# Seven half products for eight in the second net's first multiplication, with all lead times planned anew

## The chip, the cores and the metric

The kernel runs on one core of a Trainium2 chip. The metric is the device time of one execution, in microseconds (us). Three runs of the kernel before gave 726.67, 730.49 and 735.12 us, a median of 730.49.

## The reference, cut to what matters

Attention, then two feed-forward nets, on 4 x 576 = 2304 tokens of width 512:

```
out_d     = attention on means of 4 tokens, repeated 4 times
out_local = attention within |i - j| < 4
x = (out_up + out_local), heads side by side          # 2304 x 512

h = x @ w_in                                          # first net, 512 -> 2048
x = (h * tanh(softplus(h))) @ w_out                   # 2048 -> 512

h  = x @ w_in2                                        # second net, 512 -> 1024
e  = exp(h - max(h)); sm = e / (sum(e) + 1e-9)
s  = h * sm
ln = (s - mean(s)) / sqrt(var(s) + 1e-6) * g_ln
out = ln @ w_out2                                     # 1024 -> 512
```

The weights come as 64-bit floats, everything else as 32-bit.

## The kernel before, in words

**Numbers in two parts.** Every large multiplication splits both operands into a high part that the fast multiplication format holds exactly and the rest (ScalarE copies the high part, VectorE subtracts it from the whole), and adds three of the four partial products (`PASS`). So one 128 x 128 x 512 block costs three matmuls.

**First net.** Tokens go in five blocks of 3 or 4 units of 128 (`BLOCKS`). For each block 16 chunks of 128 hidden features run, one per slot: `chunk_in` (12 matmuls, then a chain of ScalarE and VectorE operations, L659 to L676) and `chunk_out` (12 matmuls into `y`, L687). The attention of later blocks runs beside the chunks of earlier ones (`coarse` for the means of 4, `local` for the band; `NEXT` gives their lead). A block's result goes to DRAM (`block_end`, `yscr`). There are 80 slots.

**Second net's weights.** `second_decode` (16 parts of 128 x 512: the first eight are w_in2, the others w_out2 with `g_ln` multiplied in) unpacks the 64-bit words, and writes a part to DRAM (`wscr`). `second_split` loads two parts and splits them into a buffer with the tag `wi`; the eight buffers of that tag come free as the first net's weights are used for the last time, in the last block.

**Second net.** It runs over 18 tiles of 128 tokens. `tile_in` loads a tile's input from `yscr` (512 features over 128 partitions in 4 parts), splits it, and does 24 matmuls (4 parts x 2 halves of 512 outputs x 3 passes, L728) into one buffer of two PSUM banks (`y`). Then: maximum (L752), exponential with its sum (L754), product with h and its sum (L757, two halves), sum of squares (L765), a few values per token (L768 to L780), scaling (L793 on VectorE, L795 on ScalarE), a turn of the 128 x 1024 result by way of DRAM (`zscr`, one write and four reads) and VectorE's transposition of 32 x 32 blocks (L821), split (L824, L825). `tile_out` does 24 matmuls (8 parts x 3 passes, L837), copies the result out (L842) and stores it. A tile takes two buffers of the tag `wo`, of which there are eight: `ez` from the exponential to the split, `ln` from the split to the end of `tile_out`. Tiles 0 and 1 do their first multiplication beside the last block's chunks. The last tile is turned by TensorE (L804) in place of DRAM.

**The order.** `Plan` collects every operation with its engine, an estimated duration, a due time in slots (`want`), and what it reads and writes. `Plan.run` then plays the queues through with these estimates: whenever an engine is free, the operation with the lowest due time whose inputs and buffers are there is taken. A due time is thus a rank and holds nothing back. The order found is written into the program; each engine works it off in sequence, waiting where an input is not there. The numbers at the top of the file (`LEAD`, `EARLY`, `WANT`, `NEXT`, ...) set the due times. SP's queue carries most transfers, GpSimd's (POOL) the averaging loads of `coarse` and the adding writes of `block_end`.

```
dma(want + 0.2, lambda: wscr[i], x, r=[x], w=[wparts[i // 2]], nbytes=262144)
...
pe(24 * 0.216, s + (8 if t < 2 else G2LAG), g2, [ln] + [w4t[k][0] for k in range(8)], [o])
```

Of the kernel before, what the change touches and what calls it, by code (L numbers as in the profile page):

```python
# [47 lines left out]
LAG = 0.15  # L48
AHEAD = 2
# [40 lines left out]
class Plan:  # L90
# [30 lines left out]
    def run(self):  # L121
# [18 lines left out]
        while len(order) < len(ops):  # L140
            for eng, queue in ready.items():
                while at[eng] <= now:
# [22 lines left out]
                    if eng in ("sp", "pool"):  # L165
                        at[eng] = now + (0.45 if eng == "sp" else 1.1)
# [4 lines left out]
                        end = dma + ((1.3 if now < 150 else 4.0) if lag is None else lag)  # L171
# [37 lines left out]
def kernel(  # L209
# [47 lines left out]
    wscr = dr.tile([16, 128, 512], F32, name="wscr")  # L257
    zscr = dr.tile([NTI, 128, 1024], F32, name="zscr")
    yparts = [[Buf(None, None, None, 0) for _ in range(2)] for _ in range(NB)]
    wparts = [Buf(None, None, None, 0) for _ in range(8)]  # L260
# [15 lines left out]
    def pe(cost, want, fn, r, w, after=()):  # L276
        return op("pe", cost, want, fn, r, w, after=after)
# [337 lines left out]
    w3t = {}  # L615
    w4t = {}
# [18 lines left out]

    def second_split(j, want):
        w = S([128, 2, 2, 512], "wi", 8, F32R)
# [72 lines left out]
    def tile_in(t, s):  # L710
# [7 lines left out]
        dma(s - 2, xf, lambda: yscr[:, :, 128 * t:128 * t + 128], r=yparts[i] + ([] if first else yparts[NB - 2]) + wparts, w=[xf, x], nbytes=262144)  # L718
# [3 lines left out]
        for m in range(2):  # L722
# [8 lines left out]
            pe(12 * 0.216, s, g1, [x] + [w3t[c, m][0] for c in range(4)], [hs[m if first else 0]])  # L731
# [3 lines left out]
        zv = View(ez, lambda b: b[:, 0].rearrange("p (a f) -> p a f", a=4))  # L735
        zs = Buf(None, None, None, 0)
        e = lambda: ez()[:, 0].rearrange("t (m f) -> t m f", m=2)
        mv = S([128, 4], "mv", 2)
        r = S([128, 4], "r2", 2)
# [16 lines left out]
        for m in range(2):  # L756
# [31 lines left out]
        def turned(m):  # L788
# [4 lines left out]
        dve(dve_us(512), s + 0.4, lambda: nc.vector.tensor_scalar(  # L793
            turned(0), flat(0), mv()[:, 2:3], y(), op0=ALU.add, op1=ALU.mult), [mv, r], [ez])
        act(act_us(512), s + 0.4, lambda: nc.scalar.activation(  # L795
            turned(1), flat(1), AF.Identity, bias=c(), scale=y()), [r], [ez])
# [16 lines left out]
        dma(s + 0.5, lambda: zscr[t], lambda: ez()[:, 1], r=[ez], w=[zs], nbytes=524288, lag=0.3)  # L813
        for g in range(4):
            dma(s + 0.6, lambda g=g: zv()[32 * g:32 * g + 32],
                lambda g=g: zscr[t].rearrange("(a t) (g f) -> g t a f", a=4, g=4)[g],
                r=[zs, ez], w=[zv], nbytes=131072, join=True, lag=1.0)
# [11 lines left out]
    def tile_out(t, s, ln):  # L829
# [23 lines left out]
    dve(0.1, -99, lambda: nc.vector.memset(ones()[:, 1:2], 0.5), [], [ones])  # L853
    for t in sms:
# [55 lines left out]
    for k in range(8):  # L910
        second_split(k, 16 * NB - 16 + 2 * k + 2)
    for t in range(NTI):
        s = 16 * NB + (INTO[t] if t < 2 else 3 * (t - 2))
        tile_out(t, s, tile_in(t, s))
# [70 lines left out]
```

## Time and profile before

| | |
|---|---|
| median of 3 runs | 730.49 us (726.67 to 735.12) |
| profiled execution | 731.2 us, span 729.4 us |
| mean granted TensorE clock | 0.979 |
| TensorE matmul busy | 692.7 us (95%), 5584 instructions |
| VectorE busy | 458.0 us (63%) |
| ScalarE busy | 489.9 us (67%) |
| GpSimd busy | 71.3 us (10%) |
| mean transfer rate | 135 GB/s |

The span is the time from the first to the last instruction of one execution. Busy times of engines overlap. The first net with its attention fills the span to about 538 us; the second net's tiles the rest.

### The profile page before, as it was taken

Reading aid. Unit: us, or ns where it says so; the run is one execution under the profiler, and the core shown is the slowest. Engines: PE = TensorE matmul, PEld = TensorE weight load, DVE = VectorE, ACT = ScalarE, POOL = GpSimd, SP = SyncE. Lnnn points to the kernel's source line nnn. Section 1 sums busy time; section 2 is a strip of 40 time slices with the busy share of each in tenths; the row PEclk is TensorE's granted clock in tenths of the full one; section 3 lists DMA queues with packets and bytes.
Section 4 is the critical chain, followed back from the end, with each engine's and each line's share of the span. In section 5 each row is a group of like instructions: output and inputs, shape, how many; then the busy total and the mean of one; then the engine's idle time right before and its main releaser. Section 6 shows DMA issues by size and latency. Waiting matters only on the chain.

```text
span 729.4 us, 14381 instructions
## 1 busy us (share of the span) xinstructions
PE 692.7 (95%) x5584; PEld 583.3 (80%) x5584; DVE 458.0 (63%) x1008; ACT 489.9 (67%) x1159; POOL 71.3 (10%) x86
## 2 busy tenths in 40 slices
PE   3748999999999998999999999999999999999997
PEld 2546778999987787999778888888888788888886
DVE  6597987787655454655665647445556667667662
ACT  3877987887878675666776757677655555555552
POOL 2042351122311121000000000000000000000000
PEclk9959999999999998999999999999999999999999
DMA  8897875847445355242343323312234544444331
GB/s 250 250 235 201 233 183 114 269 107 170 90 106 139 76 123 135 86 153 75 108 134 96 105 73 113 119 44 85 75 111 120 173 162 142 143 161 136 129 126 44
DMA packets 75564, 98.35 MB, mean 135 GB/s; under 512 B 6568, under 2 KB 58152, under 8 KB 75496
## 3 DMA queue, kind: packets, MB, share of 16 engines
q1 hardware_dynamic: 63464, 83.61, 36.3%
q0 software_dynamic: 9440, 9.10, 8.9%
q10 hardware_dynamic: 2592, 4.72, 1.7%
q8 instruction: 44, 0.72, 0.4%
q14 instruction: 24, 0.20, 0.1%
HBM read 73.81 MB, written 23.59 MB: 134 GB/s over the span
## 4 chain that ended last, share of the span: by engine, by line
PE 84%; DMA 6%; DVE 3%; SPq 2%; ACT 2%; issue 1%; POOL 0%; POOLq 0%; ACTq 0%
PE y L687 26%; PE h L659 25%; PE at L837 13%; PE y L728 12%; DMA qkd<-in_qkc_dram 3%; SPq L268 2%; PE at L420 2%; PE at L728 1%; DMA qu<-in_qu_dram 1%; PE at L490 1%; PE at L358 1%; DMA vd<-in_vc_dram 1%; PE at L397 1%; PE at L539 1%; PE at L526 1%
## 5 line engine op out<-in xcount | busy, mean ns | idle before, releaser
L687 PE MATMUL y<-g,wo 128*128 128x512 f32 (+1 forms) x960 | 219.1, 376 | 0.0
L659 PE MATMUL h<-x,wi 128*128 128x512 f32 (+1 forms) x960 | 213.4, 373 | 2.1 <-DVE e L673 2.1
L659 PEld LDWEIGHTS h<-x,wi 128*128 128x128 f32 x960 | 174.2, 189 | 26.8 <-DVE e L673 3.3
L687 PEld LDWEIGHTS y<-g,wo 128*128 128x128 f32 x960 | 173.9, 190 | 24.4 <-issue 2.0
L837 PE MATMUL at<-wi,wo 128*128 128x512 f32 x432 | 100.6, 389 | 0.0
L837 PEld LDWEIGHTS at<-wi,wo 128*128 128x128 f32 x432 | 81.0, 188 | 16.8
L728 PE MATMUL y<-wi,raw 128*128 128x512 f32 x384 | 89.9, 390 | 1.1 <-DVE raw L720 1.1
L728 PEld LDWEIGHTS y<-wi,raw 128*128 128x128 f32 x384 | 71.9, 188 | 16.6 <-DVE raw L720 1.5
L667 ACT ACTIVATE e<-h 128x512 f32<-128x512 f32 (+1 forms) x80 | 44.2, 552 | 59.5 <-PE h L659 59.0
L673 DVE SCALAR_TENSOR_TENSOR e<-e,h 128x512 f32<-128x512 f32 (+1 forms) x80 | 50.3, 629 | 34.4 <-ACT e L672 33.9
L669 ACT ACTIVATE e<-e,ones 128x512 f32<-128x512 f32 (+1 forms) x80 | 54.5, 681 | 19.5 <-DVE e L668 18.9
L668 DVE TENSOR_SCALAR e<-e 128x512 f32<-128x512 f32 (+1 forms) x80 | 31.9, 399 | 51.7 <-ACT e L667 51.5
L676 DVE TENSOR_TENSOR g<-e,g 128x512 fp32r<-128x512 f32 (+1 forms) x80 | 50.7, 634 | 19.9 <-ACT g L675 19.1
L675 ACT CAST g<-e 128x512 fp32r<-128x512 f32 (+1 forms) x80 | 46.0, 574 | 24.3 <-DVE e L673 23.9
L671 ACT ACTIVATE e<-e,ones 128x512 f32<-128x512 f32 (+1 forms) x80 | 54.4, 680 | 1.7
L266 POOL DMA_DIRECT2D qkd<-in_qkc_dram x36 | 35.4, 1017 | 147.1 <-DMA qkd<-in_qkc_dram 77.7
L672 ACT ACTIVATE e<-e 128x512 f32<-128x512 f32 (+1 forms) x80 | 46.8, 585 | 1.1
L266 POOL DMA_DIRECT2D vd<-in_vc_dram x36 | 35.4, 1030 | 50.7 <-DMA vd<-in_vc_dram 45.9
L842 ACT COPY ys<-at 128x512 f32<-128x512 f32 x18 | 10.6, 589 | 38.5 <-PE at L837 38.5
L379 ACT ACTIVATE sm<-sm,nm 128x40 f32<-128x40 f32 x112 | 35.1, 316 | 0.7 <-DVE nm L373 0.6
L754 ACT ACTIVATE wo<-y,nm 128x1024 f32<-128x1024 f32 x16 | 17.9, 1118 | 22.3 <-DVE nm L752 22.3
L554 DVE TENSOR_SCALAR ys<-ys 128x512 int32<-128x512 int32 (+1 forms) x38 | 18.8, 495 | 19.7 <-ACT ys L553 19.3
(166 smaller groups left out, 803.0 us busy)
## 6 DMA issues: line engine op xcount, KB each, us to landing
raw<-in_w_dram SPq DMA_DIRECT2D x24, 512.0 KB
zscr<-wo SPq DMA_DIRECT2D x17, 512.0 KB
wo<-zscr SPq DMA_DIRECT2D x68, 128.0 KB
qkd<-in_qkc_dram POOLq DMA_DIRECT2D x36, 144.0 KB, 4.4
wi<-in_w_dram SPq DMA_DIRECT2D x5, 1024.0 KB
wo<-in_w_dram SPq DMA_DIRECT2D x5, 1024.0 KB
ku<-in_ku_dram SPq DMA_DIRECT2D x15, 320.0 KB
vu<-in_vu_dram SPq DMA_DIRECT2D x60, 80.0 KB
```

The source lines that it names most:

```text
L266: return op("pool", nbytes / DMA_RATE, want, lambda: nc.gpsimd.dma_start(out_(), in_(), accum_op=ALU.add), r, w, after=after)
L659: mm(h()[:, :N], w()[:, f % 2, a, 128 * c:128 * c + 128], x()[:, b, c, :N], start=(n == 0), stop=(n == 11))
L667: act(act_us(N), s + 0.1, lambda: nc.scalar.activation(e(), h()[:, :N], AF.Exp), [h], [eb])
L669: act(act_us(N, 0.09), s + 0.1, lambda: nc.scalar.activation(e(), e(), AF.Square, bias=ones()[:, 0:1]), [ones], [eb])
L671: lambda: nc.scalar.activation(e(), e(), AF.Ln, scale=0.5, bias=ones()[:, 1:2]), [ones], [eb])
L672: act(act_us(N), s + 0.1, lambda: nc.scalar.activation(e(), e(), AF.Exp, scale=-1.0), [], [eb])
L673: dve(dve_us(N), s + 0.2, lambda: nc.vector.scalar_tensor_tensor(e(), e(), 1.0, h()[:, :N], op0=ALU.subtract, op1=ALU.mult), [h], [eb])
L675: act(act_us(N), s + 0.2, lambda: nc.scalar.copy(g()[:, 0, :N], e()), [eb], [g])
L676: dve(dve_us(N), s + 0.2, lambda: nc.vector.tensor_tensor(g()[:, 1, :N], e(), g()[:, 0, :N].bitcast(F32), op=ALU.subtract), [eb], [g])
L687: mm(y[d2]()[:, d, :N], w()[:, f % 2, a, c:c + 128], g()[:, b, :N], start=(f == fs[0] and n == 0), stop=(f == fs[-1] and n == 2))
L728: mm(part(m), x()[:, a, c, :], w()[:, i, b, :], start=(n == 0), stop=(n == 11))
L837: mm(o(), ln()[:, a, k, :], w()[:, i, b, :], start=(n == 0), stop=(n == 23))
```

## The change

Tiles 2 to 15 are taken in pairs (`PAIRED`). Tile t is `xa`, tile t + 1 `xb`, the input features are cut into two halves and the outputs into two halves, so that a pair's first multiplication is a 2 x 2 by 2 x 2 product of blocks: eight half products, each 128 tokens x 256 features x 512 outputs, 6 matmuls. `pair_in` does it with seven (Strassen's scheme in Winograd's form): four sums of the inputs, four of the weights, seven products in four banks (both banks of a `y` buffer and both `h` banks), and sums of the products. Two of the products are added onto banks that hold an earlier product, after that one has been read.

- `weight_sums` makes the four sums of w_in2's blocks, in two halves, and writes them to `wscr` as eight more parts. `second_split` then runs for 12 pairs of parts; `HOMES` puts eight into `wi`, two into `wo` (of eight buffers) and two into the buffer `x0` of the first net's input, `SPLITS` gives order and due times.
- `pair_in` splits seven operands of 256 features (four blocks of input, of which two as one copy and one alone, and four sums). For every second pair, the first among them, they lie in `x1`, the input buffer of the last block; for the others in `raw`, `e` and `vu`. The results of the products are added into `c2` in SBUF, two by plain additions, four by an addition that also keeps the maximum. Exponential and product then read SBUF and not PSUM, 1024 wide; the second tile of a pair has later due times (`PSTEP`).
- `normal` is the rest of `tile_in`, now shared. The square of the scaled sum goes from VectorE (two operations) to ScalarE (one). In pairs both scalings are ScalarE's.
- `tile_out` takes its output buffer from `qu` and `ku`, and a lag of its own for the tiles of a pair (`PLAG`).
- The planner's estimates: TensorE 0.2267 us for a matmul of the second net in place of 0.216, 0.05 us more for any group on TensorE, 0.47 us more for a GpSimd transfer, other lags for the turn through DRAM. All numbers that set due times are new.

```
-LEAD = 2.2
-EARLY = -95.5
-CLOAD0 = -108.6
-VLOAD = [-115.1, -87.3]
-LOAD0 = -77.4
-FIRST = {'wi': (-67.7, -66.3), 'wo': (-64.9, -40.0)}
...
-NEXT = {0: (0.6, 7.5, -8.4, 0.2), 26: (-4.7, 4.4, -13.4, 0.2), 32: (-3.9, 7.5, -5.0, 1.7), 48: (1.4, 10.4, 2.8, 3.4)}
-WANT = [6.9, 4.6, 4.5, 5.8, -4.5, 13.8, 34.8, 28.7]
-G2LAG = 10
-INTO = (-7, -0.9)
+LEAD = 2.22
+EARLY = -97.3
+CLOAD0 = -101.34
+VLOAD = [-107.17, -83.16]
+LOAD0 = -80.26
+FIRST = {'wi': (-68.45, -50.57), 'wo': (-67.01, -47.07)}
...
+NEXT = {0: (0.03, 8.7, -23.77, 0.71), 26: (-3.98, 6.49, -13.57, 0.59), 32: (-3.63, 9.6, -1.34, 1.76), 48: (2.15, 11.88, 21.41, 28.49)}
+WANT = [11.64, 4.76, 5.17, 6.13, -17.51, 32.44, 46.22, 39.82]
+G2LAG = 35.66
+SUMS = (-4.62, 4.1)
+HOMES = ["wi"] * 6 + ["wo"] * 2 + ["x0"] * 2 + ["wi"] * 2
+SPLITS = ((8, -20.07), (9, -11.82), (0, -10.66), (1, -12.07), (2, -24.69), (3, 0.53), (10, 20.13), (11, 5.71), (6, 2.55), (7, 32.54), (4, -88.28), (5, 21.64))
+PAIRED = range(2, 16, 2)
+PLAG = (16.26, 16.41)
+XLOAD = -17.27
+XPREP = -37.01
+PSTEP = 45.84
+TERMS = [(0, 0, "11", False), (1, 5, "T2", False), (2, 3, "T3", False), (3, 4, "T1", False),
+         (0, 1, "21", False), (3, 6, "22", True), (2, 2, "T4", True)]
+INTO = (-26.71, -0.78)
+POOL_LAG = 0.47
...
-        return op("pe", cost, want, fn, r, w, after=after)
+        return op("pe", cost + 0.05, want, fn, r, w, after=after)
...
+    def weight_sums(c, want):
+        xs = [S([128, 2, 512], tag, 1) for tag in ("vu", "atT")]
+        for h in range(2):
+            dma(want - 2, xs[h], lambda h=h: wscr[2 * c + 4 * h:2 * c + 4 * h + 2].rearrange("i k n -> k i n"),
+                r=[wparts[c], wparts[c + 2]], w=xs, nbytes=524288, join=h > 0)
...
+        for out_, i0, i1 in (...):
+            dve(dve_us(512), want, lambda ...: nc.vector.tensor_tensor(
+                out_(), i0(), i1(), op=ALU.subtract), [], [a, b])
+        for h in range(2):
+            j = 8 + 2 * c + h
+            dma(want + 0.2, lambda j=j: wscr[2 * j:2 * j + 2].rearrange("i k n -> k i n"), xs[h], r=[xs[h]], w=[wparts[j]], nbytes=524288)
...
+    def pair_in(t, s, loads):
+        xp = S([128, 2, 4, 128], "ys", 2)
+        sums = S([128, 4, 2, 128], "atT", 1)
+        if t % 4 == 2:
+            x = S([128, 7, 2, 2, 128], "x1", 1, F32R)
+            cuts = [(0, 2), (2, 3), (3, 7)]
...
+        else:
+            cuts = [(0, 2), (2, 3), (3, 5), (5, 7)]
...
+        for o, i0, i1, f in (...):
+            dve(dve_us(256), s - XPREP, lambda ...: nc.vector.tensor_tensor(
+                sums()[:, o], i0(), i1(), op=f), xs, [sums])
+        for (a, b), home in zip(cuts, homes):
...
+            act(act_us(256 * (b - a)), s - XPREP, lambda src=src, home=home: nc.scalar.copy(home()[:, :, 0], src()), [buf], [home])
+            dve(dve_us(256 * (b - a)), s - XPREP, lambda src=src, home=home: nc.vector.tensor_tensor(
+                home()[:, :, 1], src(), home()[:, :, 0].bitcast(F32), op=ALU.subtract), [buf], [home])
...
+        yt = P("y")
+        banks = [View(yt, lambda b, m=m: b[:, m]) for m in range(2)] + [P("h"), P("h")]
+        def product(n, k, name, more):
...
+                for c in range(2):
+                    for a, b in PASS:
+                        w, m = ws[c]
+                        mm(banks[n](), home()[:, o, a, c, :], w()[:, m, b, :], start=(i == 0 and not more), stop=(i == 5), skip_group_check=more)
+                        i += 1
+            pe(6 * 0.2267, s, g1, [home] + [w for w, _ in ws], [banks[n]])
+        c2 = [S([128, 2, 512], "g", 3) for _ in range(2)]
...
+        def plus(out_, a, n, r=None, m=0, first=True):
+            if r is None:
+                dve(dve_us(512) + 0.1, s + 0.1, lambda: nc.vector.tensor_tensor(out_(), a(), banks[n](), op=ALU.add), [a, banks[n]], [out_])
+            else:
+                dve(dve_us(512) + 0.1, s + 0.1, lambda: nc.vector.tensor_tensor_reduce(
+                    out_(), a(), banks[n](), 1.0, LOWEST if first else r()[:, 1:2], ALU.add, ALU.max,
+                    r()[:, 1:2] if first else r()[:, 2:3]), [a, banks[n]], [out_, r])
...
+        go()
+        act(act_us(512), s + 0.1, lambda: nc.scalar.copy(ct[0](), banks[0]()), [banks[0]], [ct[0]])
+        go()
+        plus(u, ct[0], 1)
+        go()
+        plus(cu[1], u, 2)
+        go()
+        plus(cu[1], cu[1], 3, nms[1])
+        go()
+        plus(ct[0], ct[0], 0, nms[0])
+        go()
+        plus(ct[1], u, 3, nms[0], first=False)
+        go()
+        plus(cu[0], u, 2, nms[1], first=False)
+        for n in range(2):
+            nm, h, hs = nms[n], c2[n], (ct, cu)[n]
+            d = PSTEP * n
...
+            act(act_us(1024, 0.2), s + 0.2 + d, lambda ...: nc.scalar.activation(
+                ez()[:, 0], hv(), AF.Exp, bias=nm()[:, 0:1], accum_out=su()[:, 0:1]), hs + [nm], [ez, su])
+            dve(dve_us(1024) + 0.1, s + 0.3 + d, lambda ...: nc.vector.tensor_tensor_reduce(
+                ez()[:, 0], ez()[:, 0], hv(), 1.0, 0.0, ALU.mult, ALU.add, mv()[:, 0:1]), hs, [ez, mv])
...
+            lns.append(normal(t + n, s + d, ez, su, mv))
+        return lns
...
-            pe(12 * 0.216, s, g1, [x] + [w3t[c, m][0] for c in range(4)], [hs[m if first else 0]])
+            pe(12 * 0.2267, s, g1, [x] + [w3t[c, m][0] for c in range(4)], [hs[m if first else 0]])
...
-    def tile_out(t, s, ln):
+    def tile_out(t, s, ln, lag=None):
...
-        pe(24 * 0.216, s + (8 if t < 2 else G2LAG), g2, [ln] + [w4t[k][0] for k in range(8)], [o])
-        os_ = S([128, 512], "ys", 2)
+        pe(24 * 0.2267, s + (lag or (8 if t < 2 else G2LAG)), g2, [ln] + [w4t[k][0] for k in range(8)], [o])
+        os_ = S([128, 512], ("qu", "ku")[t % 2], 1)
...
-    for k in range(8):
-        second_split(k, 16 * NB - 16 + 2 * k + 2)
+    for c in range(2):
+        weight_sums(c, 16 * NB - 16 + SUMS[c])
+    for j, want in SPLITS:
+        second_split(j, 16 * NB - 16 + want)
```

## Rows read from the trace of the kernel before

**Rows 1.** Busy time by stretch: start:end, length, busy (instructions) by engine, clock, transfers.

```profile
0.00:125.00 125.00, 95.51 (x1288) 74.54 (x1289) 97.05 (x194) 92.82 (x280) 37.28 (x48) 0.90 0.80 214
...
520.00:729.40 209.40, 204.57 (x905) 168.66 (x903) 129.02 (x333) 107.69 (x202) 0.00 (x0) 1.00 0.39 128
```

**Rows 2.** The chain of waits in order of time: start, length, what.

```profile
588.75 5.44 PE y L728 x24
594.19 5.44 PE at L837 x24
...
714.75 10.93 PE at L837 x48
```

**Rows 3.** Busy time by stretch, two tiles of the steady part.

```profile
621.39:643.15 21.76, 21.76 (x97) 18.02 (x97) 14.49 (x38) 11.60 (x22) 0.00 (x0) 1.00 0.44 146
```

**Rows 4.** Groups by line and shape, 520 us on: busy, mean ns, idle before.

```profile
L757 DVE SCALAR_TENSOR_TENSOR wo<-wo,y 128x512 f32<-128x512 f32 x32 | 21.8, 681 | 4.4 <-ACT wo L754 3.8
...
L752 DVE TENSOR_REDUCE nm<-y 128x1 f32<-128x1024 f32 x16 | 19.6, 1222 | 10.8 <-PE y L728 10.7
...
L795 ACT ACTIVATE wo<-wo,r 128x512 f32<-128x512 f32 x17 | 13.9, 816 | 15.2 <-DVE r L780 15.0
...
L793 DVE TENSOR_SCALAR wo<-wo,mv,r 128x512 f32<-128x512 f32 x17 | 9.2, 539 | 0.0
...
L720 DVE TENSOR_TENSOR raw<-ku,raw 128x512 fp32r<-128x512 f32 x8 | 5.5, 690 | 1.7 <-ACT raw L719 1.7
L719 ACT CAST raw<-ku 128x512 fp32r<-128x512 f32 x8 | 4.9, 607 | 0.0
...
L772 ACT ACTIVATE r<-r 128x1 f32<-128x1 f32 x17 | 3.4, 201 | 0.9 <-DVE r L768 0.9
...
L757 DVE DVE_READ_ACCUMULATOR wo<-wo,y 128x1 f32 x32 | 2.6, 83 | 0.0
...
L762 DVE TENSOR_SCALAR su<-su 128x1 f32<-128x1 f32 x17 | 2.5, 149 | 0.0
L563 DVE TENSOR_TENSOR wi<-ys,wi 128x1024 fp32r<-128x1024 f32 x2 | 2.4, 1222 | 0.3 <-ACT wi L562 0.3
L562 ACT CAST wi<-ys 128x1024 fp32r<-128x1024 f32 x2 | 2.1, 1044 | 0.0
```

**Rows 5.** Groups of VectorE by line and shape, whole run.

```profile
L430 DVE TENSOR_TENSOR ys<-at,up 128x256 f32<-128x256 f32 x20 | 8.1, 420 | 9.5 <-PE at L420 9.2
...
L558 DVE SCALAR_TENSOR_TENSOR ys<-wi,ys 128x1024 int32<-128x1024 int32 x5 | 6.1, 1229 | 0.0
```

**Rows 6.** Instructions in order of time, one tile: start, length, what.

```profile
628.13 1.12 ACT L754 ACTIVATE wo<-y,nm 128x1024 f32<-128x1024 f32 x1 [1.25 <-DVE nm L752]
...
648.02 0.62 ACT L824 CAST wo<-wo 128x512 fp32r<-128x512 f32 x1 [0.26 <-DVE wo L821]
...
651.80 0.68 DVE L825 TENSOR_TENSOR wo<-wo 128x512 fp32r<-128x512 f32 x1
...
659.31 5.60 PE L837 MATMUL at<-wi,wo 128*128 128x512 f32 x24
```

**Rows 7.** Busy time by stretch, the last block of the first net.

```profile
420.00:540.00 120.00, 119.97 (x529) 98.81 (x528) 65.02 (x120) 81.76 (x134) 0.00 (x0) 1.00 0.25 80
```

**Rows 8.** Instructions of TensorE in order of time, where the nets meet.

```profile
527.25 5.60 PE L728 MATMUL at<-wi,raw 128*128 128x512 f32 x24
...
538.13 5.72 PE L728 MATMUL y<-wi,raw 128*128 128x512 f32 x24
```

**Rows 9.** One instruction of TensorE and its wait; busy time of the stretch.

```profile
278.68 1.22 PE L490 MATMUL at<-qkd 64*64 64x144 f32 x12 [2.19 <-DMA qkd<-in_qkc_dram]
...
276.00:292.00 16.00, 13.80 (x133) 12.34 (x132) 7.05 (x18) 8.79 (x31) 2.50 (x3) 0.79 0.49 124
```

**Rows 10.** Instructions of TensorE in order of time: the first large matmuls.

```profile
54.38 7.12 PE L659 MATMUL h<-x,wi 128*128 128x512 f32 x24
```

**Rows 11.** Waits from 520 us on: engine, line, for whom, total, times, longest.

```profile
DVE r L768 <- ACT wo L765: 31.7, 16, 2.5
```

More of the change, by code (lines that the diff above doesn't have):

```diff
@@ L170, in run @@
                         dma = max(dma, at[eng] + 1.2) + cost
-                        end = dma + ((1.3 if now < 150 else 4.0) if lag is None else lag)
+                        end = dma + (((1.3 if now < 150 else 4.0) + (POOL_LAG if eng == "pool" else 0.0)) if lag is None else lag)
                     else:
@@ L256 @@
     yscr = dr.tile([128, 4, NT], F32, name="yscr")
-    wscr = dr.tile([16, 128, 512], F32, name="wscr")
+    wscr = dr.tile([24, 128, 512], F32, name="wscr")
     zscr = dr.tile([NTI, 128, 1024], F32, name="zscr")
     yparts = [[Buf(None, None, None, 0) for _ in range(2)] for _ in range(NB)]
-    wparts = [Buf(None, None, None, 0) for _ in range(8)]
+    wparts = [Buf(None, None, None, 0) for _ in range(12)]
     def dma(want, out_, in_, r=(), w=(), nbytes=0, accum=False, after=(), pool=False, join=False, lag=None):
@@ L615 @@
     w3t = {}
+    wsum = {}
+    xsum = S([128, 2, 2, 2, 512], "x0", 1, F32R)
     w4t = {}
@@ L711, in tile_in @@
+    def tile_in(t, s, loads):
         i = max(n for n in range(NB) if starts[n] <= 128 * t)
@@ L717, in tile_in @@
         part = (lambda m: hs[m]()) if first else (lambda m: hs[0]()[:, m, :])
-        dma(s - 2, xf, lambda: yscr[:, :, 128 * t:128 * t + 128], r=yparts[i] + ([] if first else yparts[NB - 2]) + wparts, w=[xf, x], nbytes=262144)
+        dma(s - 2, xf, lambda: yscr[:, :, 128 * t:128 * t + 128], r=yparts[i] + ([] if first else yparts[NB - 2]) + wparts, w=[xf, x], nbytes=262144, after=loads[-1:])
         act(act_us(512), s - 1, lambda: nc.scalar.copy(x()[:, 0], xf()), [xf], [x])
@@ L791, in turned @@
             return ez()[:, 1].rearrange("t (g k f) -> t g k f", g=4, k=8)[:, :, 4 * m:4 * m + 4]
[L793 to L796, printed above, removed]
+        paired = t in PAIRED or t - 1 in PAIRED
+        if not paired:
+            dve(dve_us(512), s + 0.4, lambda: nc.vector.tensor_scalar(
+                turned(0), flat(0), mv()[:, 2:3], y(), op0=ALU.add, op1=ALU.mult), [mv, r], [ez])
+        for m in range(0 if paired else 1, 2):
+            act(0.82, s + 0.4, lambda m=m: nc.scalar.activation(
+                turned(m), flat(m), AF.Identity, bias=c(), scale=y()), [r], [ez])
         if last:
@@ L909 @@
         second_decode(k, s, [g1_op[s]])
-    for k in range(8):
-        second_split(k, 16 * NB - 16 + 2 * k + 2)
+    for c in range(2):
+        weight_sums(c, 16 * NB - 16 + SUMS[c])
+    for j, want in SPLITS:
+        second_split(j, 16 * NB - 16 + want)
+    for n in ("11", "21", "22"):
+        for c in range(2):
+            wsum[n, c] = w3t[c + 2 * (n[0] == "2"), int(n[1]) - 1]
+    loads = []
     for t in range(NTI):
         s = 16 * NB + (INTO[t] if t < 2 else 3 * (t - 2))
-        tile_out(t, s, tile_in(t, s))
+        if t not in PAIRED and t - 1 not in PAIRED:
+            tile_out(t, s, tile_in(t, s, loads))
+        elif t in PAIRED:
+            lns = pair_in(t, s, loads)
+            for n in range(2):
+                tile_out(t + n, s, lns[n], PLAG[n])
     plan.run()
```

97 lines of the change are left out of this document (78 added, 19 removed).

## The prediction

> **What bounds the kernel now.** I read the busy table by stretch first. In the opening (0 to 125 us) TensorE works 95.51 of 125 us; in the second net (520 us to the end) it works 204.57 of 209.40 us, at a granted clock of 1.00, the 2.4 GHz level [rows 1]. Of the 4.83 us left there, 3.7 lie after the last matmul (714.75 + 10.93 = 725.68 to 729.4) and only 1.1 us in the stage itself [rows 1, 2]. The chain of waits says the same: in the second net it is an unbroken alternation of TensorE groups, 24 matmuls in 5.44 us, first and second multiplication in turn [rows 2]. One matmul thus costs 5.44 / 24 = 0.2267 us, and each one taken away shortens the run by that, as long as the other engines keep up. For those I read two tiles of the steady part: in 21.76 us VectorE is busy 14.49 us and ScalarE 11.60 us [rows 3]. There is room, but it is what the change spends.
>
> **What the change removes.** Tiles 2 to 15 become seven pairs. A pair needed 2 x 24 matmuls for its first multiplication and needs 7 x 6 = 42. Saved: 7 x 6 x 0.2267 = 9.5 us, all on the path. A pair's share of TensorE falls from 21.76 to (42 + 48) x 0.2267 = 20.40 us. Tiles 0, 1, 16 and 17 stay as they were, so the ending (last second multiplications, copy, store) costs what it did.
>
> **VectorE per pair.** Gone are two maxima (1.22 each), two splits of the input (0.69), four multiply-and-sum (0.68 and 0.08 to read the sum), two scalings (0.54) and four small steps (0.15) [rows 4]: 2.44 + 1.38 + 3.06 + 1.08 + 0.60 = 8.6 us. New are four sums of half width; the nearest row is a 128x256 addition, 0.42 [rows 5]: 1.7 us. The split of seven half-wide operands, as 512 + 256 + 1024 (0.69 + 0.42 + 1.22) or with 1024 in two halves, costs 2.4 [rows 4, 5]. Of six additions that take the products out of PSUM, two are plain (0.69) and four also carry a maximum. No row shows that form; the nearest is the multiply-and-sum with one operand in PSUM, 0.68 + 0.08 [rows 4]: 4.4 together. Then, per tile, one multiply-and-sum over 1024 with both operands in SBUF (no row shows that either; 1.22 + 0.08 by the 1024-wide rows) and a sign change (0.15): 2.9. In all 11.4, and VectorE goes from 14.49 to 17.3 of 20.40 us, from 67% to 85%. ScalarE loses two copies (0.61) and gains the copies of the seven operands (0.61 + at most 0.61 + 1.04, or four smaller: 2.3), one copy out of PSUM (0.6), two small squares (about 0.2 each) and two scalings (0.82) [rows 4]: 11.60 - 1.2 + 4.9 = 15.3, 75%. Both stay below TensorE.
>
> How fast the two unseen forms are is the open price. As far as the rows go, a 1024-wide operation with two SBUF operands and no sum takes 1.23 us, and one with a sum and a PSUM operand takes 0.68 us for 512: neither is slowed [rows 4, 5]. So I take full speed; the other end is half speed. [...]
>
> **Waits that the pair adds.** Product six accumulates onto the bank that product four filled, and so waits for the addition that reads it. Product four ends at 4 x 1.36 = 5.44 us in the pair, its addition about 0.9 later, product five at 6.80: half a microsecond of margin, less than one wide VectorE operation (1.22) that may stand ahead in VectorE's queue. Behind product six stand all later matmuls of TensorE's queue. Product five needs the ScalarE copy of the first bank, four products old: free. The two buffers of the softmax and the transposed result: in the trace one is held from the exponential at 628.13 to 652.5, the other from 648.02 to 664.9 [rows 6], 24.4 + 16.9 us per tile; two tiles in 20.40 us fill 4.0 buffers on average, and there are now six, since two keep weights. SP's queue holds as many entries per two tiles as before. For new gaps on TensorE I take +1.5 us over the seven pairs, near the 1.1 us that the stage shows now, with 0 and 6.4 (rival B) as ends.
>
> **The extra weights.** Eight subtractions (0.69) and four more splits (1.22 on VectorE, 1.04 on ScalarE) are 10.4 and 4.2 us [rows 4], and twelve more transfers of 512 KB. They lie beside the last block of the first net: from 420 to 540 us VectorE is idle 55 of 120 us, ScalarE 38, the transfer engines are busy a quarter of the time [rows 7]. Cost 0; were the last split late, 2.3. The first pair's operands lie in the buffer of the last block's input, free after the last matmul of the first layer, at 527.25. Behind it TensorE has the first multiplication of tile 1 and the last products of the block, until 538.13: 10.9 us [rows 8] against some 4.5 us of copies and splits. Cost 0; without that cover, up to 4.5.
>
> **The new lead times.** They set the order of all queues, from the first load on. Two places can move. At 276.5 TensorE waits 2.19 us for the averaged keys and queries of a batch, then works at a lowered clock; from 276 to 292 the mean granted clock is 0.79, between the 1.2 and the 2.4 GHz level, and 21% of 16 us is 3.4 us [rows 9]. Those averages are four transfers of GpSimd's queue in a row, and the plan now allows each 0.47 us more: 1.9 us, nearly the wait. A plan that sees it can put other matmuls there: between -5.6 and +2 (the wait doubled), I take -3. The opening has 29.5 us of idle TensorE, and its first large matmul starts at 54.38 [rows 1, 10]; loads and unpacking change places there in both senses (the second half of the first weights is asked for later, the first loads of the units earlier). No row says which way it goes: 0, with a fifth of the idle, 6 us, to either side.
>
> **Sum.** The profiled execution took 731.2 us (span 729.4 and 1.8 around it), 0.7 above the median of the runs shown. 731.2 - 9.5 + 1.5 - 3.0 + 0 = 720.2, and I say 720 (716 to 724 if the case is right).
>
> **Rivals.** B: VectorE waits as it waits now. In the second net it stood still 31.7 us, 16 times, some 2.0 us a tile, for ScalarE's sum of squares [rows 11]. Were that to stay, a pair would cost VectorE 17.3 + 2 x 2.0 = 21.3 us against 20.40: 7 x 0.9 = 6.4 us, 725. For it: at 85% the margin is thin, and the order is fixed in advance. Against: in two tiles VectorE now has 7.3 us to spare, so that nothing needed to be put into that wait.
>
> C: the opening turns out 6 us later: 726. D: 6 us earlier: 714. Neither has a row for it beyond the idle.
>
> E, the other side: the 1024-wide multiply-and-sum on two SBUF operands runs at half speed. From 512 to 1024 is 0.54 us more [rows 4], so half speed is 1.22 + 2 x 0.54 = 2.3 us, 1.08 more per tile; VectorE's pair is then 19.5, and with its waits 23.5 us, 3.1 over TensorE's: 21.5 us, about 740. It decides as soon as VectorE's work and waits together pass 20.40. Against it speak the two rows at full speed; for it, that no row joins the two properties. [...]
>
> **How the numbers follow.** Forecast 0.50, B 0.20, C 0.12, D 0.08, E 0.10. A measurement here tells 1% from no change: below 723.2 counts as faster, above 737.8 as slower. Faster: 0.85 of the forecast's half, all of D, a fifth of B and C: 0.43 + 0.08 + 0.06 = 0.57. Slower: E, 0.10. The rest 0.33. The range runs from 712, below D, to 732, above B and C with some of their spread; it leaves out E and the outer parts of C and D, 2 in 10.
>
> **What would show it.** Right: 42 matmuls for 48 in each pair at 0.2267 us; gaps of a few tenths before product six; VectorE near 85% in a pair; no wait near 276 us. B: TensorE waiting in every pair for VectorE, which waits for ScalarE. E: the wide reduction above 2 us. C and D: the first large matmul far from 54.4 us, or other idle time before 125 us. The forecast is wrong most easily through the opening, which these rows can't order.

## The result, and the profile after

The changed kernel takes **724.23 us** (median of 14 runs, 721.93 to 725.31) against 730.59 us for the kernel before in the same runs (14 runs, 726.67 to 736.56): a ratio of 0.9905, with an interval from 0.9883 to 0.9927. It is 6.4 us faster. That is clear of noise, but just under 1%, above the 723.2 us below which the prediction speaks of faster; it lies inside the range of 712 to 732 and 4 us above the forecast. The profiled execution took 725.31 us (span 723.5, clock 0.979), the longest of the 14 runs, against 731.2.

What the change took away is in the page's busy table (busy us, share of the span, instructions): 42 matmuls fewer than the 5584 of before, while VectorE and ScalarE have 24.4 and 25.5 us more to do.

```profile
PE 687.7 (95%) x5542; PEld 575.9 (80%) x5542; DVE 482.4 (67%) x1051; ACT 515.4 (71%) x1212; POOL 71.4 (10%) x86
```

The busy table by stretch of the kernel after, with the columns of [rows 1]. The first and the last row answer to [rows 1], the third, some three and a half pairs, to [rows 3], the second to [rows 9].

```profile
0.00:125.00 125.00, 98.53 (x1275) 75.78 (x1276) 94.53 (x192) 92.07 (x278) 37.36 (x48) 0.88 0.80 211
276.00:292.00 16.00, 15.98 (x223) 14.53 (x222) 12.69 (x33) 14.20 (x45) 5.36 (x7) 1.00 0.80 182
582.04:655.00 72.96, 71.89 (x316) 58.82 (x315) 61.24 (x161) 53.64 (x106) 0.00 (x0) 1.00 0.51 163
520.00:723.50 203.50, 196.33 (x863) 160.49 (x862) 145.48 (x366) 130.22 (x256) 0.00 (x0) 1.00 0.42 136
```

In the third row VectorE is busy 84% and ScalarE 74%. From 520 us on, TensorE stands idle 7.17 us where it stood 4.83. Some 4.0 of the 7.17 lie after the last matmul (719.5 us), so about 3.2 lie inside the stage, which had 1.1. The stretch from 276 to 292 us has lost its wait, and its clock is 1.00.

TensorE's waits in the kernel after, from 440 us on (engine, what, line, for whom: total, times, longest). In the kernel before the same view has one line of 1.1 us.

```profile
PE h L698 <- DVE e L712: 1.3, 1, 1.3
PE h L798 <- DVE g L810: 1.3, 1, 1.3
PE y L798 <- ACT vu L743: 0.8, 1, 0.8
PE y L798 <- ACT g L823: 0.7, 1, 0.7
PE h L798 <- DVE nm L812: 0.4, 1, 0.4
```

This view leaves out that the first matmul behind a wait is itself slower to pass: at the five waits described below, the next one starts 0.337 to 0.341 us behind it. Counted by what the starts of successive matmuls lie apart beyond 0.2267 us, from 478 us to the last matmul, the kernel after loses **6.1 us** and the kernel before **1.6**. This count, called lost time below, is what goes beside the medians.

The chain of waits of the kernel after, in order of time (start, length, what), for [rows 2]:

```profile
653.32 1.36 PE h L798 x6
654.67 2.72 PE y L798 x12
...
664.20 10.88 PE at L987 x48
```

10.88 / 48 = 0.2267 us a matmul, in the second multiplication as in the products (1.36 / 6).

The groups of VectorE by line and shape, from 520 us on (busy, mean ns of one, idle before and its releaser), for [rows 4]:

```profile
L847 DVE CUSTOM_DVE_ANT_0 wo<-wo,g 128x1024 f32<-128x1024 f32 x14 | 16.9, 1220 | 3.7 <-ACT wo L845 3.7
L812 DVE CUSTOM_DVE_ANT_0 g<-e,h,nm 128x512 f32<-128x512 f32 x14 | 10.1, 732 | 0.1
L812 DVE CUSTOM_DVE_ANT_0 g<-g,h 128x512 f32<-128x512 f32 x7 | 4.8, 683 | 0.3 <-ACT wo L845 0.3
L812 DVE DVE_READ_ACCUMULATOR2_ANT nm<- 128x1 f32 x28 | 2.3, 83 | 0.0
```

L847 is the wide multiply-and-sum with both operands in SBUF: 1.220 us. L812 is the addition with a maximum: 0.683 us, or 0.732 where the maximum starts from an earlier one, each with 0.083 to read the result.

The waits of VectorE from 520 us on, for [rows 11]:

```profile
DVE wo L971 <- DMA wo<-zscr: 10.2, 11, 1.7
...
DVE r L915 <- ACT wo L912: 4.3, 4, 1.4
```

The wait for ScalarE's sum of squares fell from 31.7 to 4.3 us. In its place VectorE's transposition (L971) waits for the reads of the turn through DRAM: 10.2 us in 11 waits, where the kernel before had 2.6 in 2.

### The profile page after: what moved, and what is told of

Same layout as the page of the kernel before. It is cut to its first block, busy times and chain, and to the rows that moved or that the text cites. A ratio compares the mean times of both kernels' runs of the same rounds, so it can differ in the third digit from the quotient of the medians.

```text
span 723.5 us, 14419 instructions
## 1 busy us (share of the span) xinstructions
PE 687.7 (95%) x5542; PEld 575.9 (80%) x5542; DVE 482.4 (67%) x1051; ACT 515.4 (71%) x1212; POOL 71.4 (10%) x86
## 4 chain that ended last, share of the span: by engine, by line
PE 81%; DMA 6%; ACT 4%; DVE 4%; SPq 4%; issue 1%; POOL 0%; ACTq 0%; DVEq 0%; POOLq 0%
PE h L698 27%; PE y L726 25%; PE at L987 11%; SPq L281 4%; PE h L798 3%; PE y L798 3%; PE at L433 2%; PE at L872 2%; PE y L872 2%; DMA qu<-in_qu_dram 1%; PE at L503 1%; PE at L371 1%; PE at L539 1%; DMA qkd<-in_qkc_dram 1%; PE at L552 1%
## 5 line engine op out<-in xcount | busy, mean ns | idle before, releaser
L698 PE MATMUL h<-x,wi 128*128 128x512 f32 (+1 forms) x960 | 216.6, 377 | 6.4 <-DVE e L712 4.0
L698 PEld LDWEIGHTS h<-x,wi 128*128 128x128 f32 x960 | 176.3, 191 | 32.7 <-DVE e L712 5.7
L726 PEld LDWEIGHTS y<-g,wo 128*128 128x128 f32 x960 | 171.8, 188 | 26.2 <-issue 2.2
L712 DVE SCALAR_TENSOR_TENSOR e<-e,h 128x512 f32<-128x512 f32 (+1 forms) x80 | 50.5, 632 | 40.7 <-ACT e L711 40.0
L987 PE MATMUL at<-wi,wo 128*128 128x512 f32 x216 | 52.0, 390 | 0.0
L987 PE MATMUL at<-wo 128*128 128x512 f32 x216 | 51.9, 389 | 0.0
L987 PEld LDWEIGHTS at<-wo 128*128 128x128 f32 x216 | 40.5, 188 | 8.4
L987 PEld LDWEIGHTS at<-wi,wo 128*128 128x128 f32 x216 | 40.5, 188 | 8.4
L974 ACT CAST wo<-wo 128x512 fp32r<-128x512 f32 x34 | 21.0, 617 | 26.2 <-DVE wo L971 18.5
L971 DVE STREAM_TRANSPOSE wo<-wo 128x512 f32<-128x512 f32 x34 | 23.9, 706 | 10.2 <-DMA wo<-zscr 10.2
L975 DVE TENSOR_TENSOR wo<-wo 128x512 fp32r<-128x512 f32 x34 | 23.2, 686 | 8.7 <-ACT wo L974 8.1
```

What stands on the lines that cost most here:

```text
L698: mm(h()[:, :N], w()[:, f % 2, a, 128 * c:128 * c + 128], x()[:, b, c, :N], start=(n == 0), stop=(n == 11))
L712: dve(dve_us(N), s + 0.2, lambda: nc.vector.scalar_tensor_tensor(e(), e(), 1.0, h()[:, :N], op0=ALU.subtract, op1=ALU.mult), [h], [eb])
L726: mm(y[d2]()[:, d, :N], w()[:, f % 2, a, c:c + 128], g()[:, b, :N], start=(f == fs[0] and n == 0), stop=(f == fs[-1] and n == 2))
L987: mm(o(), ln()[:, a, k, :], w()[:, i, b, :], start=(n == 0), stop=(n == 23))
```

## Where TensorE waits now

Two stretches of the kernel after, instructions in order of time (start, length, engine, what, and in brackets the idle time before it and its releaser). The first lies in a pair:

```profile
577.76 0.71 DVE L971 STREAM_TRANSPOSE wo<-wo 128x512 f32<-128x512 f32 x1 [1.13 <-DMA wo<-zscr]
578.39 0.11 DVE L849 TENSOR_SCALAR mv<-mv 128x1 f32<-128x1 f32 x1
578.43 0.67 DVE L810 TENSOR_TENSOR g<-e,h 128x512 f32<-128x512 f32 x1
579.15 0.98 PE L798 MATMUL h<-x,x 128*128 128x512 f32 x3 [1.26 <-DVE g L810]
```

One of the last two products (product seven, which the plan put ahead of product six here) is to be added onto a bank that the addition L810 must read first. That addition stands in VectorE's queue behind a transposition of another tile, and this one is held 1.13 us by its transfer. VectorE stands still with work behind it, and TensorE stands still behind VectorE (1.5 us of lost time). The wait at 609.84 us has the same head: a transposition that waited 1.66 us at 606.83.

The second stretch lies in the last block of the first net:

```profile
486.16 1.03 ACT L575 CAST wi<-ys 128x1024 fp32r<-128x1024 f32 x1
487.23 1.23 DVE L576 TENSOR_TENSOR wi<-ys,wi 128x1024 fp32r<-128x1024 f32 x1 [0.48 <-ACT wi L575]
488.37 0.68 DVE L712 SCALAR_TENSOR_TENSOR e<-e,h 128x512 f32<-128x512 f32 x1
489.10 3.01 PE L698 MATMUL h<-x,wi 128*128 128x512 f32 x12 [1.31 <-DVE e L712]
```

A split of weights, 1.23 us in one piece and itself kept waiting for ScalarE's half, stands ahead of a chunk's operation that frees a bank `h`: 1.6 us of lost time. The other two places: at 542.02 us the first pair waits for the bank that ScalarE copies at the end of the last block (L743; 1.1 us), and at 636.65 us product five waits for ScalarE's copy of the first bank (L823; 0.95 us):

```profile
633.09 1.52 PE L798 MATMUL y<-wi,raw 128*128 128x512 f32 x6
...
635.13 0.84 PE L798 MATMUL y<-wi,vu 128*128 128x512 f32 x3
636.01 0.59 ACT L823 COPY g<-y 128x512 f32<-128x512 f32 x1 [0.81 <-PE y L798]
...
636.65 1.66 PE L798 MATMUL y<-wi,raw 128*128 128x512 f32 x6 [0.68 <-ACT g L823]
```

Here the plan took products one, two and five in a row, at 633.09, 634.45 and 636.65 us; three and four follow at 643.59. ScalarE was idle for 0.81 us before the copy and began it 0.04 us after the end of product two, though the copy reads only product one's bank. The two banks are one buffer `y`; that the copy waits for the whole buffer is inferred from these times.

## The experiments

Theory: the pairs save 9.5 us, the replan gives little, and the rest of the shortfall is TensorE's new waits, which come from the order in VectorE's queue. Rivals: VectorE is too full, whatever the order; or the new opening costs what the pairs save. The experiments ran in three lots, each with runs of the kernel before beside it (medians 729.16, 729.05 and 729.02 us, against 730.59 above), and ratios are to those; times of different lots can be 1.5 us apart for that alone.

**The replan without the pairs.** The kernel before with the new numbers of the first net and the new estimates, tiles still single.

```
 kernel before
-LEAD = 2.2 ... WANT = [6.9, ...]
+LEAD = 2.22 ... WANT = [11.64, ...]     # LEAD to CLOAD, NEXT, WANT as in the change
-INTO = (-7, -0.9); G2LAG = 10
+INTO = (-3.4, 0.5); G2LAG = 14.8
-        return op("pe", cost, want, fn, r, w, after=after)
+        return op("pe", cost + 0.05, want, fn, r, w, after=after)
...     # GpSimd's 0.47, 0.2267 a matmul, due times of the eight splits
```

> No pairs: the kernel before with the changed kernel's numbers and estimates for the first net, and due times of the second net set for single tiles. Theory (the new order of the first net gives nothing by itself, the pairs give 9.5 us less the waits they bring): 730 us, 729 to 732, no wait of 2 us near 276 us but as much more lost before 260 us. Rival (the new order gives the 3 us I forecast, and the pairs only 3 to 4): 727 us.

Measured: 728.68 us against 729.16, ratio 0.9993 (0.9976 to 1.0009). The replan alone is worth 0.5 us, within its interval of none. Its lost time after 478 us is 1.3 us. From here 728.7 - 9.5 (matmuls) + 4.8 (lost time, 6.1 - 1.3) = 724.0. The kernel after took 724.23 in the first lot and, beside a kernel before of nearly the same median as here, 723.66 further down; by the ratios the pairs are worth 4 to 6 us where the sum says 4.7.

**The old opening under the pairs.**

```
 kernel after
-LEAD = 2.22 ... WANT = [11.64, ...]; POOL_LAG = 0.47
+LEAD = 2.2 ... WANT = [6.9, ...]; POOL_LAG = 0.0     # LEAD to CLOAD, NEXT[0], WANT as before
```

> Pairs kept, but the numbers that order the opening (and the extra allowance of 0.47 us for GpSimd's transfers) are those of before. Theory (the old opening is the better one: up to 260 us the kernel before had lost 2.7 us less on TensorE): 721 to 722 us. Rival (the openings cost the same, or the new one is better with the new estimates): 724 to 727 us.

Measured: 725.7 us, ratio 0.996 (0.994 to 0.998). The kernel after was not in this lot; its ratios in two others, 0.9905 and 0.9935, put the old opening 2 to 4 us behind. The new opening is not what eats the gain; if anything it is the better one beside the pairs.

**Honest lags for the turn.** The plan reckons that the write to DRAM lands 0.9 us before its modelled end and the reads 0.3 us after (in the kernel before it was 0.3 and 1.0 us after). Here both come 1.5 us later:

```
 kernel after
-        dma(s + 0.5, ... zscr[t] ..., lag=-0.9)
+        dma(s + 0.5, ... zscr[t] ..., lag=0.6)
-                ..., join=True, lag=0.3)
+                ..., join=True, lag=1.8)
```

> The changed kernel with one thing else: the plan allows the turn through DRAM 1.5 us more for the write and 1.5 us more for the reads, so VectorE's transpositions are put later in its queue. Theory (TensorE's new waits of 2 to 3 us come from additions of the products that stand behind a transposition waiting for its transfer): VectorE waits under 4 us for those transfers instead of 10.2, TensorE's waits in the pairs go from 3.2 to about 1, 722 us. Rival (VectorE is simply too full at 85%): the waits stay, 724 us.

Measured: 724.05 us, ratio 0.9916 (0.9894 to 0.9939), which the kernel after's 0.9905 and 0.9935 enclose: no gain. VectorE's wait for the reads all but went, in the waits from 520 us on:

```profile
DVE wo L971 <- DMA wo<-zscr: 1.1, 1, 1.1
```

but TensorE's lost time went only from 6.1 to 5.6 us. The waits of TensorE in this kernel, from 440 us on:

```profile
PE h L698 <- DVE e L712: 1.3, 1, 1.3
PE y L798 <- ACT vu L743: 0.8, 1, 0.8
PE y L798 <- ACT g L823: 0.7, 1, 0.7
PE h L798 <- DVE nm L812: 0.4, 2, 0.3
PE h L798 <- DVE g L810: 0.2, 1, 0.2
```

The long wait behind L810 is down to 0.2 us; those for L712, L743 and L823 don't depend on the turn and stay, and small ones came. The theory that this wait is the shortfall fell: it is one of several.

**Order, not load.** The lags of the last experiment, the twelve splits of weights in halves of 512, and the due times of the second net set anew (the additions out of the banks 8 slots ahead of their products in rank, the transpositions later):

```
 kernel after
-        split(w, x, want)
+        for m in range(2):
+            act(act_us(512), want + 0.1, lambda m=m: nc.scalar.copy(w()[:, m, 0], x()[:, m]), [x], [w])
+        for m in range(2):
+            dve(dve_us(512), want + 0.1, lambda m=m: nc.vector.tensor_tensor(
+                w()[:, m, 1], x()[:, m], w()[:, m, 0].bitcast(F32), op=ALU.subtract), [x], [w])
...
-(additions and copy out of the banks)  s + 0.1
+                                       s + -8.03
-(transposition)                        s + 0.9
+                                       s + 4.68
-XLOAD, XPREP, INTO[0] = -17.27, -37.01, -26.71
+XLOAD, XPREP, INTO[0] = -31.15, -23.5, -25.59     # and six numbers of SPLITS and PLAG
```

> The changed kernel with the longer turn allowances, the twelve splits of the second net's weights in halves of 512 (so that none stands 1.2 us ahead of a chunk's operations), and the second net's due times set anew; matmuls and VectorE's work as they were. Theory (the waits are a matter of what stands ahead in VectorE's and ScalarE's queues): TensorE's waits after 480 us fall from 5.9 to about 1, 719 to 721 us. Rival (at 85% VectorE is the bound, whatever the order): the waits come up elsewhere, 724 us.

Measured: **720.36 us** (719.02 to 721.48), ratio 0.9879 (0.9835 to 0.9922), and in a second lot, under the expectation that follows, **720.15 us** (718.88 to 720.53), ratio 0.9877 (0.985 to 0.9903). It beats both kernels. Lost time: 1.5 us.

> The retuned kernel again, unaltered, as the measure for the next two on the same chip: 720 to 721 us.

Its only wait of TensorE from 440 us on, and its busy time by stretch (from the first lot):

```profile
PE y L802 <- ACT g L827: 0.7, 1, 0.7
```

```profile
520.00:700.00 180.00, 179.32 (x792) 147.50 (x791) 144.09 (x375) 126.80 (x254) 0.00 (x0) 1.00 0.47 150
582.00:655.00 73.00, 72.32 (x318) 59.20 (x317) 61.15 (x160) 54.94 (x108) 0.00 (x0) 1.00 0.48 155
```

VectorE is as full as in the kernel after (61.15 of 73.00 us), with TensorE busy 179.32 of 180. So the 84% alone costs nothing. The one wait that is left is product five's again: products one, two and five stand in a row (622.25, 623.61 and 625.81 us in the second lot's profile).

The kernel after, once more beside it:

> The changed kernel again, unaltered, so that the next two are compared on the same chip: 724 us, 0.990 of before. Its first net has the order of the run with longer turn allowances; the idle time of TensorE up to 440 us differed by 2 us between those two profiles, and should differ as much here if that is chance and not the order.

Measured: 723.66 us, ratio 0.9935 (0.991 to 0.9961), lost time 5.9. Up to 450 us the order on TensorE, VectorE and ScalarE is the same in the traces of the kernel after, the one with longer lags and the retuned one. Even so TensorE was idle up to 440 us for 27.3 and 26.5 us in two profiles of the kernel after, 28.1 with the longer lags, and 30.1 and 26.9 in two of the retuned kernel. What differs there is chance and not the order (the 2 us of the expectation are 0.8 by these busy times).

**More load on VectorE.** One more 1024-wide multiplication per tile of a pair, whose result nothing uses:

```
 kernel after, in pair_in
+            dve(dve_us(1024), s + 0.3 + d, lambda ez=ez, hv=hv: nc.vector.tensor_tensor(
+                ez()[:, 1], hv(), hv(), op=ALU.mult), hs, [ez])
```

> The changed kernel with one idle multiplication of 128x1024 on VectorE more per tile of a pair, 2 x 1.22 us a pair, in the plan too; results unchanged. It is what half speed of the wide multiply-and-sum would have cost. Theory (VectorE has some 3 us of room per pair, and a planned order can use nearly all): 725 to 727 us. Rival (my price for that case, where VectorE's waits of 2 us a tile stay): about 740 us.

Measured: 728.61 us, ratio 0.9991 (0.996 to 1.0022), 5 us over the kernel after: more than the theory's 725 to 727, far from the rival's 740. Lost time: 10.3 us. 2 x 1.22 us a pair make 19.8 of 20.40 us, and the busy table shows VectorE at 93% in the stretch that stood at 84%:

```profile
582.00:655.00 73.00, 70.58 (x301) 57.53 (x302) 67.72 (x168) 51.65 (x100) 0.00 (x0) 0.98 0.49 160
```

A good part of the loss is one event, in the waits of TensorE, in order of time and in the busy table:

```profile
PE h L798 <- DVE g L810: 3.5, 2, 3.1
```

```profile
579.16 0.71 DVE L973 STREAM_TRANSPOSE wo<-wo 128x512 f32<-128x512 f32 x1 [1.27 <-DMA wo<-zscr]
...
579.84 1.21 DVE L849 TENSOR_TENSOR wo<-g 128x1024 f32<-128x1024 f32 x1
...
582.96 0.65 DVE L810 TENSOR_TENSOR g<-e,h 128x512 f32<-128x512 f32 x1
...
583.66 1.16 PE L798 MATMUL h<-x,x 128*128 128x512 f32 x3 [3.12 <-DVE g L810]
```

```profile
583.00:588.00 5.00, 4.34 (x12) 3.46 (x13) 4.91 (x14) 3.10 (x5) 0.00 (x0) 0.66 0.29 114
```

A wait of 3.1 us, and behind it a mean granted clock of 0.66, between the 0.50 and the 1.00 that the clock has in the trace of the kernel before (last section): 12 matmuls in the five us (0.66 of them still the wait) in place of 22. Ahead of the addition L810 stand both the added multiplication (L849, 1.21 us) and a transposition held 1.27 us by its transfer. So the load costs something in this order, with its short lags; how much of it load alone would cost is not shown, since the multiplication was not added to the retuned kernel.

**Which part of the new order does it.** The retuned kernel with one part put back: first the short lags of the turn, then the whole splits of 1024.

```
 retuned kernel, first
-lag=0.6 (write), lag=1.8 (reads)
+lag=-0.9,        lag=0.3
```

> The retuned kernel with the changed kernel's short allowances for the turn through DRAM put back, all else as retuned. If the wrong allowances cost what the waits behind transpositions suggest: VectorE waits some 8 to 10 us for those reads again, TensorE 1 to 2 us, 722 us. If only what stands right ahead of the additions matters: 720 to 721 us.

Measured: 726.31 us (723.77 to 729.38), ratio 0.9969 (0.9947 to 0.9991): 6.2 us slower than the retuned kernel in the same lot, lost time 7.2. The waits of VectorE for the reads are back, where the retuned kernel has none, and the longest wait of TensorE has its old cause (the waits from 520 us on, then instructions in order of time):

```profile
DVE wo L975 <- DMA wo<-zscr: 8.1, 11, 1.7
```

```profile
640.60 0.71 DVE L975 STREAM_TRANSPOSE wo<-wo 128x512 f32<-128x512 f32 x1 [0.97 <-DMA wo<-zscr]
...
642.14 0.69 DVE L979 TENSOR_TENSOR wo<-wo 128x512 fp32r<-128x512 f32 x1
...
642.74 0.68 DVE L814 TENSOR_TENSOR g<-e,h 128x512 f32<-128x512 f32 x1
...
643.48 0.96 PE L802 MATMUL h<-x,e 128*128 128x512 f32 x3 [2.03 <-DVE g L814]
```

So the lags, which gave nothing by themselves, are worth 6 us where the rest of the order is right. The edit moves two estimates, but the plan then found another order for TensorE, VectorE and ScalarE from 536 us on (by the traces), and the 6 us are the price of that order. Both answers of the expectation were too low, and the profile (723.77 us) is of the shortest of 12 runs.

```
 retuned kernel, second
-(splits of 512), SPLITS (3, -5.52), XLOAD = -31.15, XPREP = -23.5
+split(w, x, want), SPLITS (3, 0.53), XLOAD = -17.27, XPREP = -42.98     # XPREP of neither kernel
```

> The retuned kernel with the twelve splits of the second net's weights in one piece of 1024 again (and the due times that go with that). Theory (the wait near 488 us, 1.6 us, comes of a 1.2 us split standing ahead of a chunk's operation, and of nothing else): that wait comes back alone, 722 us. Rival (it comes of the changed order of the whole last block): no such wait, 720 us.

Measured: 723.25 us, ratio 0.9924 (0.9903 to 0.9945): 3.1 us slower, lost time 4.8. The wait behind the whole split is there again (1.6 us at 488.23, `h` for L712); the rest is a handful of small waits in the pairs, so it did not come back alone. The two put-backs, 6.2 and 3.1 us, add up to more than the 3 to 4 us that the new order gains: each makes the plan anew. The third part, the earlier rank of the additions, was not put back by itself.

Over these kernels lost time and median go together: 1.5 us with 720.15 and 720.36; 4.8 with 723.25; 5.6, 5.9 and 6.1 with 724.05, 723.66 and 724.23; 7.2 with 726.31; 10.3 with 728.61. The kernel with the old opening, 5.2 and 725.7, stands apart. Lost time is read from one execution, but it repeats: 6.1 and 5.9 in two profiles of the kernel after, 1.5 twice in the retuned one, 1.6, 1.5 and 1.5 in three of the kernel before.

**The wait at 276 us.** Two more profiles of the kernel before, unchanged.

> The kernel before, unchanged, to see a second profile of it. Theory: TensorE's wait of 2.19 us at 276 us and the lowered clock behind it belong to the planned order, so they are in every run of this kernel: the stretch from 276 to 292 us shows a clock near 0.8 again, TensorE has done some 929 matmuls of the first net's two layers by 300 us and some 1537 by 440 us, and the span is near 729 us. Then the new plan saved this wait and gave 3 us of it back elsewhere. Rival: the wait hangs on how the transfers fell in the one profiled run; then this profile shows a clock of 1.00 there, some 940 or more by 300 us, and a span of 726 to 728 us.

> The kernel before once more, a third profile. Theory (the wait at 276 us belongs to the order): clock near 0.8 from 276 to 292 us in this one too. Rival (it hangs on the run): present in some profiles and not in others, and the span goes with it by 2 to 4 us.

Measured: 728.72 us (span 726.9) and 730.68 us (span 728.9). Busy time of the opening in the execution that was predicted from, for comparison:

```profile
40.00:64.00 24.00, 15.11 (x296) 12.26 (x296) 19.19 (x41) 15.46 (x48) 11.18 (x12) 0.64 0.94 237
```

Busy time by stretch, and the instruction that waits, of the first of the two, then of the second:

```profile
40.00:64.00 24.00, 16.61 (x323) 13.46 (x319) 18.64 (x39) 14.61 (x48) 10.71 (x12) 1.00 0.94 232
276.00:292.00 16.00, 15.32 (x217) 13.96 (x216) 9.77 (x26) 12.24 (x39) 2.51 (x3) 1.00 0.59 150
...
279.04 0.95 PE L490 MATMUL at<-qkd 64*64 64x144 f32 x12 [0.53 <-DMA qkd<-in_qkc_dram]
```

```profile
40.00:64.00 24.00, 15.93 (x305) 12.92 (x303) 18.23 (x38) 13.91 (x45) 10.84 (x12) 0.57 0.95 242
276.00:292.00 16.00, 15.12 (x160) 14.04 (x159) 9.42 (x22) 12.25 (x39) 2.94 (x4) 1.00 0.72 165
...
281.37 0.95 PE L490 MATMUL at<-qkd 64*64 64x144 f32 x12 [0.88 <-ACT e L672]
```

The rival holds for the wait: the same program has 2.19 us with the lowered clock in one execution [rows 9], 0.5 us at a full clock in the next, and in the third none for this transfer (0.9 us for ScalarE). But it was less the transfer that moved than TensorE: what waits started at 278.68, 279.04 and 281.37 us, and TensorE had come to it at 276.5, 278.5 and 280.5. In the execution that was predicted from it was 2 to 4 us ahead there, and by 300 us the lead was gone (929 large matmuls against 936 and 930). Its second half, that the span goes with the wait, doesn't hold: the third profile, without the wait, has a span of 728.9 us against the 729.4 with it.

## Why the prediction was right, and what was mis-sized

- **The saved matmuls, -9.5.** Right: 42 instructions fewer at 0.2267 us each.
- **VectorE and ScalarE.** 316 matmuls of the stretch 582.04 to 655 are 3.51 pairs of 90; VectorE's 61.24 us make 17.4 a pair (17.3 were worked out) and ScalarE's 53.64 make 15.3 (as worked out). That this load fits is shown by the retuned kernel; how much more would fit is open.
- **Rival E** failed on its price: the wide multiply-and-sum on two SBUF operands takes 1.220 us in the mean of 14, what the 1024-wide operations without a sum took (1.222 and 1.229 us [rows 4, 5]). The half speed, 2.3 us, was my other end for a form without a row, and no run here shows it. The trace records this form as an instruction of another kind than the scalar-tensor-tensor form of the kernel before (0.681 us for 512, one operand in PSUM [rows 4]). No run here has the scalar-tensor-tensor form with its sum and two SBUF operands, so how fast that one is isn't shown.
- **Rival B** did not come: VectorE's wait for the sum of squares fell to 4.3 us.
- **The waits of the pair, +1.5, mis-sized.** Lost time grew by 4.5 us (6.1 - 1.6). The place was right: a product that adds onto a bank waits for VectorE's addition, and something stands ahead of it in the queue. I took a wide operation as the worst that could stand there. What stood there was a transposition waiting for its transfer, and a queue that waits has no length to be read from a row of busy times. The change had shortened the lags that the plan gives the turn, and I didn't follow that. The pair's own waits are some 3.2 us (1.5 at 579, 0.7 at 610, 0.95 at 637 us); with 1.6 at 489, 1.1 at 542 and 0.2 of crumbs they make the 6.1, and the 1.6 of before are gone.
- **"Product five needs the ScalarE copy, four products old: free."** Wrong in that pair: 0.95 us. I took the seven products to run in their order; there the plan put product five right behind product two, and the copy came between them, on an idle ScalarE. The same order of products leaves the retuned kernel its one wait.
- **The extra weights at 0.** Wrong by 1.6 us: engines idle nearly half the time still put a 1.23 us operation ahead of one that TensorE needs now. I had looked at the sum of the idle time, not at the margin of the chunk.
- **The first pair's operands at 0.** Right: no wait for them. The wait there (1.1 us) is for a bank, and the replanned kernel with single tiles has it too (1.1 us at 535 us), so it belongs to the replan and not to the pairs.
- **The replan, -3, the step that failed.** The wait did go: 276 to 292 us stands at clock 1.00. By 440 us TensorE has done 788 + 756 = 1544 matmuls of the first net's two large multiplications against 781 + 756 = 1537 in the execution from which I predicted, 7 x 0.2267 = 1.6 us. But the other two profiles of the kernel before have 792 + 756 = 1548 and 784 + 756 = 1540 by then, and the replanned kernel with single tiles 792 + 763 = 1555 (some records may be missing in any of them). I took one execution's wait for a property of the order, and its whole length for a loss, where TensorE had come to it early. Measured by medians, the replan is worth 0.5 us.
- **The opening at 0.** Not measured alone. The whole replan is worth 0.5 us without the pairs, while the old opening under the pairs costs 2 to 4. The first large matmul starts at 50.07 us in place of 54.38, and by 125 us TensorE has done 211 such matmuls against 220.

So: -9.5 + 4.8 - 0.5 = -5.2 us (4.8 is lost time against the replanned kernel with single tiles, 6.1 - 1.3, since the 0.5 holds the rest), and -6.4 was measured. The 1.2 between them lie within the interval of the ratio (0.22% of 730 us, 1.6 us) and are not explained further. The two wrong terms, some 3 us for the waits and 2.5 for the replan, have the same sign and did not cancel. The time stayed in the range because the range was wide, and it missed the narrower 716 to 724 by 0.2 us.

## What to carry to other kernels

Where a saved matmul makes other engines fuller, look at the head of the queue before the load: an operation that waits for a transfer, placed ahead of one that frees a PSUM bank, stops TensorE even where the engine is idle 16% of the time (for 1.26 us at 579 us in the kernel after). Give the planner the latency that the trace shows for every transfer that something in a shared queue waits for, cut long operations that stand beside short deadlines, and rank what frees a bank ahead of what needs it; here the three together were worth 3 to 4 us more (723.66 to 720.36 side by side). Before a wait is counted as a gain, look for it in a second profile of the same kernel, and see when the engine came to it.

## What the runs showed of the hardware

- The same program had, by the busy table from 40 to 64 us, a mean granted clock of 0.64 in the execution that was predicted from, and of 1.00 and 0.57 in the two later ones. The one at 1.00 had the shortest span (726.9 us against 729.4 and 728.9), but that the clock made it so is not shown: two more executions of the kernel before in that lot, at a mean clock of 0.998 and 0.997 over the run, took 729.82 and 728.24 us, against a median of 729.02.
- In the trace of the kernel before, the clock by the busy table is 0.50 in every microsecond from 280 to 286 us and 1.00 from 288 us on; the 0.79 of 276 to 292 us is a mean over both. By the starts of successive matmuls, one of 128x512 takes 0.427 us at 0.50 (55 us) and 0.227 at 1.00 (59 us), one of 128x384 takes 0.320 (282 us) and 0.173 (290 us). So 128 columns more cost 0.107 and 0.053 us, 1.2 and 2.4 columns a nanosecond: these are the two levels that the prediction puts in GHz.
- A wait of 3.1 us cost more than its length: behind it, the mean clock was 0.66 over 5 us, with 12 matmuls in place of 22 (583 to 588 us, 0.66 us of them still the wait, with the added multiplication). The waits of up to 1.3 us in the kernel after had no such row (its clock from 520 us on is 1.00), nor had the wait of 2.03 us at 643 us with the short lags (1.00 from 643 to 650 us).
- The fused addition with a maximum costs what a plain addition costs (0.683 to 0.732 us for 512, against 0.69), beside 0.083 us for reading the result. It and the multiply-and-sum on two SBUF operands (1.220 us for 1024) run at the speed of the plain operations (0.68 to 0.69 and 1.22 to 1.23 us).
